# Sliding-window attention and gated MLP on one core: f32 scores without a q/k split, separate rooms, and a new instruction order

## Chip, cores and metric

One core of a Trainium2 chip. The metric is the device time of one execution in microseconds. The kernel before was timed in 3 runs: 453.04 us median, 451.68 to 454.27.

## What is computed

Attention over 4 batches, 8 heads, 768 positions and 64 columns per head. Each query sees the first 4 positions (the sink) and a window of 128. Then an MLP whose gate mixes positions. Cut from the reference:

```python
# attention, q, k, v: (4, 8, 768, 64)
scores = scale * np.matmul(q, k.transpose(0, 1, 3, 2))
keep = is_sink | in_window            # k < 4, or 0 <= q - k < 128
a = softmax(where(keep, scores, -1e9))
x = matmul(a, v)                      # -> (4, 768, 512)
# MLP
h = np.maximum(x @ w_in, 0.0)         # 512 -> 1024
u, v = h[..., :512], h[..., 512:]
v_n = (v - mu) / np.sqrt(var + 1e-06)
v_s = np.einsum('ts,bsd->btd', w_spatial, v_n) + b_spatial[None, :, None]
out = (u * v_s) @ w_out
```

All inputs are f32, w_in and w_out arrive as 64-bit floats and are decoded on the chip.

## The kernel before

**Precision.** Most products keep f32 precision by splitting each operand into a high and a low part: a cast gives the high part (`high`, L567 and L569), a subtraction the low part (`low` L583, `low_scaled` L590). `three` (L601) then multiplies high by high, high by low and low by high. This serves `ps_v` and `ps_u` (x times the two halves of w_in), `ps_s` (w_spatial times the normalised v, `vn`), `ps_o` (gate times w_out) and `av` (weights times values, L926 to L928). The scores (`sc`) of batches 1 to 3 are split in the same way (L856: three products from `qp` and `kring`). Those of batch 0 are multiplied as whole f32 from the loaded q and k (L850), which the simple switch `whole(b)` with `WHOLE = 1` decides.

**Tiling.** A batch has 6 tiles of 128 queries, and each tile has two halves of 4 heads. I number the 48 halves of the program from 0: half n is batch n // 12, tile (n % 12) // 2. For each half: the scores of 4 heads go to 4 PSUM banks (`sc` has exactly 4), VectorE adds the mask and takes the row's minimum (L861), ScalarE exponentiates (L866, 4 instructions per half), the weights are cast and split into `p` (ScalarE for the high part, VectorE or GpSimd for the low), two transposes on SP's DMA queue give `pT`, TensorE multiplies by the values, VectorE divides (L934 to L936), and x is split and transposed. Then come `ps_v` with relu (L969), statistics, normalisation and split on all four engines, and `ps_u` with relu (L1017). When all six tiles of a batch have their `vn`, the twelve pieces `ps_s` of a batch can run, each followed by the gate (L1038), the product with u (L1042) and the split of g; two `ps_o` per 256 columns end it.

**Rooms.** The block `wsp` (7 x 768 f32 per partition) holds w_spatial. Before w_spatial is loaded, the first part of it holds the raw v of batch 0 (`load_v`, L427) and the rest the k of batch 0 (`k_whole`). So the loads of w_spatial (L697) wait until batch 0 has used both (keys `v0room` and `k0room`).

**Order.** Every step is a piece given to `Plan.add` with a rank (its place in the program, from the table `WHEN`), the engines that may do it (`ENGINES`), a cost, and what it reads and writes. `Plan.order` sorts by rank, takes dependencies from that sorted list, and sends each piece to an engine. The engines then execute their lists strictly in that order. SP issues all loads, transposes and stores in one such list.

```python
plan.add(r, "PE", 0.19 + n / 2 * (1.0 if whole(b) else 0.35), product, ...)   # L869: scores
high(r, "q high", 512, lambda: (qp()[:, 0], raw()[:, 0]), ...)                # L815
low(r, "q low", 512, lambda: (qp()[:, 1], raw()[:, 0], qp()[:, 0]), ...)
plan.add(max(r0 + gap * c - 1, free_at), "SP", 0.37, f, [],                   # load of w_spatial
         [("wspraw", c), ("k0room", 0)] + [("v0room", t) for t in range(NT)], ...)
```

Of the kernel before, what the change touches and what calls it, by code (L numbers as in the profile page):

```python
# [6 lines left out]
F32 = mybir.dt.float32  # L7
F32R = mybir.dt.float32r
# [36 lines left out]
def f64_to_f32(nc, raw, w, tmp, top=None):  # L45


# [171 lines left out]
def scale_from_high_word(nc, pool, top, name):  # L219
# [23 lines left out]

ENGINES = {
# [34 lines left out]
class Plan:  # L279

# [8 lines left out]
    def add(self, rank, engines, time, f, reads=(), writes=(), dma=None, shared=False):  # L289

        self.pieces.append((rank, len(self.pieces), engines, time, f, tuple(reads), tuple(writes), dma, shared))

    def order(self):
        ps = sorted(self.pieces, key=lambda x: x[:2])
        n = len(ps)
        before, seen, users, takes = [set() for _ in ps], {}, {}, {}
        for i, (_, _, _, _, _, reads, writes, _, _) in enumerate(ps):
            for key, wr in [(k, False) for k in reads] + [(k, True) for k in writes]:
                base, part = key[:2], key[2:]
                if not wr and base not in seen and base[0] != "k0room":  # L300
# [33 lines left out]
        def room(i):  # L334

            t, new = 0.0, {}
            for key in ps[i][5] + ps[i][6]:
# [7 lines left out]
                j = new[ring] = new.get(ring, 0) + 1  # L345
                ends = sorted(until[b] if b else 0.0 for b in slots[ring] if b is None or not left[b])
# [821 lines left out]
```

## Time and profile before

| | |
|---|---|
| median of 3 runs | 453.04 us (451.68 to 454.27) |
| span of the profiled execution, first to last instruction | 451.5 us |
| TensorE busy | 401.8 us, 89% of the span |
| VectorE busy | 321.7 us, 71% |
| ScalarE busy | 296.4 us, 66% |
| GpSimd busy | 206.9 us, 46% |
| mean granted TensorE clock | 0.976 |

No time of the profiled execution other than its span was recorded; the span is 1.5 us below the median of the runs. The shares are means over a program whose first third and last two thirds behave differently, so they have to be read by stretches.

### The profile page before, as it was taken

The page shows a single profiled execution, that of the slowest core. Times are in us where ns is not written, and L with a number is a line of the kernel's source. Part 1 is how long each engine was busy: PE and PEld are TensorE (multiplying, and loading weights), DVE is VectorE, ACT ScalarE, POOL GpSimd, SP SyncE. Part 2 cuts the span into 40 slices and gives each one's busy share as a digit, 9 for nine tenths or more (in the row PEclk, how much of TensorE's full clock was granted, in tenths as well). Part 3 has the DMA queues.
Part 4 walks back from the last instruction along what each step waited for, and adds up shares of the span by engine and source line. Part 5 has one row for each costly group of instructions (what it writes and reads, how often), then busy time and mean ns, then how long its engine had stood idle before and what let it go on. Part 6 is the DMA issues. An engine that isn't in the chain of part 4 may idle for free.

```text
span 451.5 us, 10014 instructions
## 1 busy us (share of the span) xinstructions
PE 401.8 (89%) x3653; PEld 306.1 (68%) x3653; DVE 321.7 (71%) x953; ACT 296.4 (66%) x639; POOL 206.9 (46%) x275
## 2 busy tenths in 40 slices
PE   2364869986977999999999999999999999999995
PEld 1243537754564798787777877877788788778883
DVE  3999978889889898859789955687988453324220
ACT  4799768899899956749898565487876342331111
POOL 4446774477588595431356544232552242102220
PEclk9999979998888999999999999999999999999999
DMA  6998799899995537647987548547743444100102
GB/s 236 334 308 207 151 167 186 215 235 267 255 207 87 113 74 204 167 123 141 228 167 177 141 104 147 140 83 185 126 98 77 120 63 108 48 23 1 47 26 75
DMA packets 142393, 66.15 MB, mean 146 GB/s; under 512 B 124545, under 2 KB 128385, under 8 KB 142337
## 3 DMA queue, kind: packets, MB, share of 16 engines
q1 hardware_dynamic: 142192, 65.44, 62.7%
q8 instruction: 30, 0.49, 0.5%
q14 instruction: 27, 0.21, 0.2%
q10 hardware_dynamic: 144, 0.00, 0.0%
HBM read 28.72 MB, written 6.29 MB: 78 GB/s over the span
## 4 chain that ended last, share of the span: by engine, by line
PE 66%; DVE 12%; DMA 8%; ACT 6%; issue 3%; POOL 3%; SPq 2%; POOLq 0%; ACTq 0%; DVEq 0%
PE ps_s L601 21%; PE ps_o L601 14%; PE ps_v L601 10%; PE ps_u L601 9%; PE sc L856 5%; DVE pexp L861 3%; DMA xT<-x 2%; DMA wsp<-qk_t 2%; ACT pexp L866 2%; PE av L926 1%; DVE vring L590 1%; PE av L928 1%; PE av L927 1%; DVE win L590 1%; DMA dec<-w_in 1%
## 5 line engine op out<-in xcount | busy, mean ns | idle before, releaser
L601 PE MATMUL ps_s<-wsp,vn 128*128 128x256 f16 x864 | 100.2, 273 | 0.0
L601 PEld LDWEIGHTS <-vn 128*128 128x128 f16 x864 | 82.9, 98 | 13.8 <-issue 2.2
L866 ACT ACTIVATE pexp<-pexp,nm 128x260 f32<-128x260 f32 (+1 forms) x192 | 80.7, 483 | 11.1 <-DVE nm L861 10.7
L601 PE MATMUL ps_v<-win,xT 128*128 128x512 f16 x288 | 70.9, 399 | 4.6 <-DMA xT<-x 3.7
L601 PE MATMUL ps_u<-xT,win 128*128 128x256 f16 x576 | 70.8, 276 | 4.0 <-ACT vr L969 4.0
L601 PE MATMUL ps_o<-wout,g 128*128 128x512 f32 x288 | 73.0, 402 | 0.0
L601 PEld LDWEIGHTS <-win 128*128 128x128 f16 x576 | 55.1, 99 | 15.2 <-issue 6.7
L583 POOL TENSOR_TENSOR g<-g,g 128x256 fp32r<-128x256 f32 x48 | 39.0, 813 | 48.3 <-ACT g L567 47.1
L601 PEld LDWEIGHTS ps_o<-wout,g 128*128 128x128 f32 x288 | 52.3, 188 | 11.8 <-POOL g L583 0.3
L583 POOL TENSOR_TENSOR x<-x,x 128x256 f16<-128x256 f32 x48 | 38.6, 804 | 39.7 <-ACT x L567 39.0
L601 PEld LDWEIGHTS <-xT 128*128 128x128 f16 x288 | 27.7, 102 | 38.2 <-issue 7.4
L567 ACT CAST p<-pexp 128x1024 f16<-128x1024 f32 (+1 forms) x80 | 52.5, 669 | 0.3
L1038 DVE SCALAR_TENSOR_TENSOR g<-ps_s,isc,b_bc 128x256 f32<-128x256 f32 x48 | 23.1, 481 | 37.4 <-PE ps_s L601 37.2
L583 POOL TENSOR_TENSOR p<-pexp,p 128x16 f16<-128x16 f32 (+2 forms) x38 | 38.2, 1011 | 24.1 <-ACT p L567 20.7
L583 DVE TENSOR_TENSOR p<-pexp,p 128x1024 f16<-128x1024 f32 (+2 forms) x42 | 44.7, 1072 | 5.7 <-ACT p L567 5.7
L850 PE MATMUL sc<-wsp,qkraw 64*128 64x260 f32 (+1 forms) x96 | 23.0, 538 | 26.9 <-DMA wsp<-qk_t 9.9
L856 PE MATMUL sc<-kring,qp 64*128 64x260 f32 (+1 forms) x432 | 39.5, 307 | 3.7 <-DVE nm L861 3.7
L928 PE MATMUL av<-vring,pT 128*128 128x65 f16 x352 | 38.9, 198 | 2.8 <-DMA pT<-p 2.8
L927 PE MATMUL av<-vring,pT 128*128 128x65 f16 x352 | 39.0, 197 | 2.3 <-DVE vring L590 2.3
L856 PEld LDWEIGHTS sc<-kring,qp 64*128 64x128 f32 x432 | 30.9, 192 | 12.7 <-DVE nm L861 5.8
L1064 ACT COPY ob<-ps_o 128x512 f32<-128x512 f32 x24 | 14.0, 585 | 38.6 <-PE ps_o L601 38.6
L926 PE MATMUL av<-vring,pT 128*128 128x65 f16 x352 | 39.4, 198 | 0.0
(123 smaller groups left out, 707.2 us busy)
## 6 DMA issues: line engine op xcount, KB each, us to landing
qkraw<-qk_t SPq DMA_DIRECT2D x18, 512.0 KB, 4.1
out<-ob SPq DMA_DIRECT2D x24, 256.0 KB, 2.3
vraw<-v_s SPq DMA_DIRECT2D x18, 256.0 KB, 4.5
dec<-w_in SPq DMA_DIRECT2D x8, 512.0 KB, 6.7
wsp<-w_sp_t SPq DMA_DIRECT2D x6, 384.0 KB, 5.0
dec<-w_out SPq DMA_DIRECT2D x4, 512.0 KB, 4.8
wsp<-qk_t SPq DMA_DIRECT2D x6, 256.0 KB, 6.9
qkraw<-qk_t SPq DMA_DIRECT2D x6, 256.0 KB, 4.3
```

What stands on the lines that cost most here:

```text
L567: nc.scalar.copy(o, x)
L583: eng[e].tensor_tensor(out=o, in0=x, in1=hi, op=ALU.subtract)
L601: nc.tensor.matmul(o, a, m, start=(i == 0), stop=(i == n - 1))
L850: nc.tensor.matmul(o, tl("qkraw", (b, t))[rows, 0, hp, :], keys(k_whole, rows), start=True, stop=True)
L856: nc.tensor.matmul(o, qp[rows, qi, hp, :], keys(kring[:, ki], rows), start=(m == 0), stop=(m == 2))
L861: nc.vector.tensor_tensor_reduce(out=po, in0=o, in1=mask, scale=-0.125, scalar=3.0e38, op0=ALU.add, op1=ALU.min, accum_out=nm()[:, h2 + q: ...
L866: nc.scalar.activation(po, po, AF.Exp, bias=nm()[:, h2 + q:h2 + q + 1], scale=-1.0)
L926: nc.tensor.matmul(o[:, h], ph, vh, start=(t < 2 and j == 0), stop=False)
L927: nc.tensor.matmul(o[:, h], ph, vl, start=False, stop=False)
L928: nc.tensor.matmul(o[:, h], pl, vh, start=False, stop=(j == nb - 1 and (t < 2 or h == HH - 1)))
L1038: nc.vector.scalar_tensor_tensor(out=g(), in0=tl("ps_s", i)[:, :TC], scalar=vals["s", "sp"][1], in1=b_bc[:, t0:t0 + TC], op0=ALU.mult, op1 ...
L1064: plan.add(r + WHEN["o copy"], "a", 0.5, lambda e: nc.scalar.copy(tl("ob", i), tl("ps_o", i)), [("ps_o", i)], [("ob", i)])
```

## The change

Six things change.

1. `WHOLE`, `whole(b)`, the ring `qp` and the pieces "q high", "q low", "k high", "k low" go. All batches multiply whole f32 q and k (L803): 4 matmuls per half in place of 12. k is loaded straight into `kring` beside the two sink columns, in rows of 128 f32; q has a ring of 4.
2. `wsp` holds nothing but w_spatial, and the raw v of batch 0 is loaded like that of the other batches, tile by tile into the ring `vraw`. The keys `v0room` and `k0room` go, and with them the wait of the loads of w_spatial.
3. `Plan` takes dependencies from the order in which the pieces are listed; the rank only sets which goes first.
4. Most casts and low parts may now be done by more engines ("ad", "dp", "adp"), and the costs of the planner change.
5. The clamp of w_out goes from GpSimd to VectorE.
6. `WHEN` is a new table of numbers, with two values for each kind of piece (batch 0 and the others).

```diff
 ENGINES = {
-    "w_in high": "ap", "w_sp high": "ap", "v high": "a", "q high": "a", "k high": "a", "p high": "a",
...
+    "w_in high": "adp", "w_sp high": "adp", "v high": "ad", "p high": "ad", "sink high": "a", "x high": "adp",
...
-    "load": 5.69, "qk": 4.2, "k": 0.07, "score": 3.76, "pair": 0.43, "mask": 0.15, "exp": 0.99, "split": 1.0,
...
+    "qk load": (-1.47, 16.37), "k sink": (12.37, 77.34), "k copy": (-2.4, -12.82), "score": (-41.06, -9.59),
...
-WHOLE = 1
...
-        for i, (_, _, _, _, _, reads, writes, _, _) in enumerate(ps):
+        for _, k, _, _, _, reads, writes, _, _ in self.pieces:
+            i = place[k]
...
-    st.wsp = pool.tile([P, (NT + 1) * S], F32, name="wsp")
...
-    st.raw_v = [st.wsp[:, 512 * t:512 * t + 512] for t in range(NT)]
...
+        rooms = const.tile([P, NT + 1, S], F32, name="wsp")
...
-        kring = const.tile([P, 2, 4, HP, SEG], F32R, name="kring")
...
+        kring = const.tile([P, 4, HP, SEG], F32, name="kring")
...
-                    eng[e].tensor_scalar(w(), w(), EXP_LOW, EXP_HIGH, op0=ALU.max, op1=ALU.min)
+                    nc.vector.tensor_scalar(w(), w(), EXP_LOW, EXP_HIGH, op0=ALU.max, op1=ALU.min)
...
-                plan.add(max(r0 + gap * c - 1, free_at), "SP", 0.37, f, [],
-                         [("wspraw", c), ("k0room", 0)] + [("v0room", t) for t in range(NT)], dma=384 / 330.0)
...
+                plan.add("w_sp load", gap * c, 0, "SP", 0.37, f, [], [("wspraw", c)], dma=384 / 330.0)
...
-                    qp = tl("qp", (b, t))
-                    for m, (qi, ki) in enumerate(((0, 0), (0, 1), (1, 0))):
-                        for o, rows in zip(os, both):
-                            nc.tensor.matmul(o, qp[rows, qi, hp, :], keys(kring[:, ki], rows), start=(m == 0), stop=(m == 2))
...
+                        nc.tensor.matmul(view(h + q)[0], tl("q", (b, t))[rows, hp, :], keys, start=True, stop=True)
...
```

What each engine has to do between the exponentials of half 9 and those of half 20 (TensorE: from the scores of half 10 to those ahead of half 21), counted in the order of instructions of each kernel:

| engine | pieces | before | after |
|---|---|---|---|
| TensorE | scores of 4 heads | 9 split, 2 whole | 11 whole |
| | `ps_v`, `ps_u`, `ps_s`, `ps_o` | 6, 15, 0, 0 | 6, 16, 8, 1 |
| | matmuls of `av` | 222 | 247 |
| ScalarE | high parts of q and k | 13 | 0 |
| | sums of w_spatial (`junk<-wsp`), of v (`junk<-vraw`) | 6, 4 | 0, 9 |
| | high parts of p (1024), vn, g | 9, 6, 0 | 7, 3, 5 |
| | relu of v | 6 | 8 |
| VectorE | low parts of q and k | 6 | 0 |
| | gates, products with u, low parts of g | 0, 0, 0 | 8, 7, 5 |
| | low parts of x, w_out, vn | 0, 0, 4 | 4, 4, 1 |
| | casts of p, vn, w_out | 0 | 8 |
| | clamps and masks of decoded weights | 3 | 8 |

In the whole program GpSimd does 5 low parts of g in place of 48, 25 of x in place of 48, none of k in place of 13, and 14 of vn in place of 4.

First place: ScalarE, around the exponentials of half 16 (batch 1, tile 2). `junk` rows are the sums of w_spatial, `qp` and `kring` the high parts of q and k. Before:

```order
L700 ACTIVATE junk,mxs<-wsp 128x768
L567 CAST qp<-qkraw 128x512
L567 CAST kring<-qkraw 128x4x128
L866 ACTIVATE pexp<-pexp,nm 128x260 x4
L567 CAST x_1544<-x 128x256
L567 CAST p_1_135<-pexp 128x1024
L656 ACTIVATE w_1632<-dec 128x512
L658 ACTIVATE wtmp<-dec 128x512
L569 ACTIVATE vring<-vraw,v_scale 128x8x64
L700 ACTIVATE junk,mxs<-wsp 128x768
L969 ACTIVATE vr<-ps_v,icv_703 128x512
```

And now:

```order
L559 ACTIVATE vring<-vraw,v_scale 128x8x64 x2
L557 CAST x_1581<-x 128x256 x2
L813 ACTIVATE pexp<-pexp,nm 128x260
L916 ACTIVATE vr<-ps_v,icv_946 128x512
L813 ACTIVATE pexp<-pexp,nm 128x260
L557 CAST p_1_134<-pexp 128x1024
L956 ACTIVATE u<-ps_u,icu_605 128x256
L813 ACTIVATE pexp<-pexp,nm 128x260
L956 ACTIVATE u<-ps_u,icu_605 128x256
L813 ACTIVATE pexp<-pexp,nm 128x260
```

The sums of w_spatial and the casts of q and k are gone from here (the sums stand ahead of half 10 now), and the exponentials of one half are no longer issued in one go.

Second place: VectorE, behind the masks of half 18 (`ISA pexp` rows, not shown). Before, small sums and a division stand there:

```order
L625 TENSOR_REDUCE allmax_1866<-ps_row 1x1
L934 TENSOR_SCALAR den<-av 128x4
L935 RECIPROCAL den<-den 128x4
L936 TENSOR_TENSOR x<-av,den 128x256
L975 BN_STATS st<-vr 128x6
L977 BN_AGGR mv<-st 128x2
L979 TENSOR_SCALAR rs<-mv 128x1
L632 COPY allmax_r<-ps_col 128x1
```

And now:

```order
L639 TENSOR_SCALAR w_1796<-w_1796 128x512
L977 SCALAR_TENSOR_TENSOR g<-ps_s,isc,b_bc 128x256
L562 CAST wout<-w_1743 128x512
L981 TENSOR_TENSOR g<-g,u 128x256
L562 CAST p_1_134<-pexp 128x1024
L977 SCALAR_TENSOR_TENSOR g<-ps_s,isc,b_bc 128x256
L573 TENSOR_TENSOR wout<-w_1743,wout 128x512
L981 TENSOR_TENSOR g<-g,u 128x256
L881 TENSOR_SCALAR den<-av 128x4
```

Gates of batch 0 (`g<-ps_s`) stand ahead of the masks of half 19, with the decoding of w_out and a cast of p between them; in the kernel before, the first gate comes behind the masks of half 20.

Third place: SP's queue near the start, ahead of the first transposes of 8 blocks. Before, only loads of q, k and v stand there:

```order
L805 DMA wsp<-qk_t 128x4x128
L595 DMA vraw<-v_s 128x512 x4
L595 DMA vsraw<-v_sink 96x260
L712 DMA b_bc<-b_sp 128x768
L890 DMA_TRANSPOSE pT<-p_0_134 128x8x128 x2
```

And now:

```order
L774 DMA kring<-qk_t 128x4x128
L585 DMA q<-qk_t 128x512
L697 DMA b_bc<-b_sp 128x768
L585 DMA q<-qk_t 128x512
L683 DMA wsp<-w_sp_t 128x768 x3
L835 DMA_TRANSPOSE pT<-p_0_133 128x8x128 x2
```

Three of the six loads of w_spatial now come ahead of those transposes, where six loads of v of batch 1 stood.

## Rows read from the trace of the kernel before

**Rows 1.** The page: busy time of the engines, and two of the lines that cut the span into 40 slices of 11.3 us (busy tenths of TensorE, granted TensorE clock).

```profile
PE 401.8 (89%) x3653; PEld 306.1 (68%) x3653; DVE 321.7 (71%) x953; ACT 296.4 (66%) x639; POOL 206.9 (46%) x275
...
PE   2364869986977999999999999999999999999995
...
PEclk9999979998888999999999999999999999999999
```

**Rows 2.** Busy time by stretch (stretch, its length, then busy us and instructions of PE, PEld, DVE, ACT, POOL, the granted clock, the DMA share and GB/s).

```profile
10.00:62.00 52.00, 29.15 (x207) 19.54 (x206) 49.93 (x158) 45.56 (x100) 31.35 (x29) 0.99 0.98 245
62.00:71.50 9.50, 9.31 (x76) 5.16 (x77) 5.62 (x22) 4.10 (x10) 4.40 (x5) 0.69 0.64 134
71.50:151.30 79.80, 66.86 (x636) 46.74 (x633) 69.59 (x195) 73.71 (x161) 54.20 (x54) 0.91 0.97 206
151.30:332.00 180.70, 180.54 (x1803) 141.91 (x1802) 145.68 (x442) 130.87 (x288) 82.28 (x111) 1.00 0.65 146
332.00:451.50 119.50, 114.33 (x935) 91.44 (x932) 48.53 (x123) 38.68 (x83) 29.81 (x44) 0.99 0.24 60
```

**Rows 3.** The chain of waits that ended last, in order of time (start us, us, what): some of its TensorE pieces.

```profile
62.19 5.32 PE ps_v L601 x12
...
152.68 9.83 PE ps_s L601 x90
...
249.40 0.93 PE sc L856 x12
...
256.53 1.97 PE ps_s L601 x18
258.50 2.80 PE ps_o L601 x12
262.15 2.59 PE ps_v L601 x12
...
269.89 1.31 PE ps_u L601 x12
...
440.61 5.73 PE ps_o L601 x24
```

**Rows 4.** ScalarE's instructions in order of time (start us, duration us, line, what, count, and in brackets the idle time before and what ended it). The exponentials of half 9 are those at 69.79, the ones of half 20 those at 149.59.

```profile
67.53 0.69 ACT L969 ACTIVATE vr<-ps_v,icv 128x512 f32<-128x512 f32 x1 [3.80 <-PE ps_v L601]
69.79 1.72 ACT L866 ACTIVATE pexp<-pexp,nm 128x260 f32<-128x260 f32 x4 [1.57 <-DVE nm L861]
...
72.06 0.62 ACT L567 CAST vn<-vr 128x512 f16<-128x512 f32 x1
72.58 1.04 ACT L567 CAST p<-pexp 128x1024 f16<-128x1024 f32 x1
73.53 0.40 ACT L567 CAST x<-x 128x256 f16<-128x256 f32 x1
...
149.59 1.71 ACT L866 ACTIVATE pexp<-pexp,nm 128x260 f32<-128x260 f32 x4
```

**Rows 5.** TensorE in order of time: two groups of whole f32 scores of batch 0 with what follows them (each f32 matmul leaves two records), and two neighbouring matmuls of `av`.

```profile
53.15 1.15 PE L850 MATMUL sc<-wsp,qkraw 64*128 64x260 f32 x8
54.23 0.28 PE L920 MATMUL av<-vsink,pT 96*128 96x260 f16 x1
...
54.87 0.19 PE L928 MATMUL av<-vring,pT 128*128 128x65 f16 x1
54.90 0.19 PE L926 MATMUL av<-vring,pT 128*128 128x65 f16 x1
...
71.80 1.15 PE L850 MATMUL sc<-wsp,qkraw 64*128 64x260 f32 x8
72.88 2.76 PE L601 MATMUL ps_v<-win,xT 128*128 128x512 f16 x12
```

**Rows 6.** VectorE's instructions in order of time.

```profile
92.28 0.68 DVE L583 TENSOR_TENSOR qp<-qkraw,qp 128x512 fp32r<-128x512 f32 x1
92.88 0.42 DVE L861 CUSTOM_DVE_ANT_0 pexp<-sc,m_second 128x260 f32<-128x260 f32 x1
...
93.22 0.43 DVE L861 CUSTOM_DVE_ANT_0 pexp<-sc,m_second 128x260 f32<-128x260 f32 x1
...
98.19 1.84 DVE L590 SCALAR_TENSOR_TENSOR vring<-vraw,v_scale,vring 128x512 f16<-128x512 f32 x1
```

**Rows 7.** GpSimd's instruction at the moment of the last of these rows.

```profile
98.22 1.26 POOL L667 TENSOR_TENSOR w<-w,wtmp 128x512 int32<-128x512 int32 x1 [1.12 <-DVE w L664]
```

**Rows 8.** Groups of instructions by line and form (count, then busy us in all, mean ns of one, idle us before them and what ended it).

```profile
L567 ACT CAST qp<-qkraw 128x512 fp32r<-128x512 f32 x18 | 11.1, 614 | 3.3 <-PE sc L856 3.3
L700 ACT ACTIVATE junk<-wsp 128x768 bf16<-128x768 f32 x6 | 5.0, 841 | 1.1 <-DMA wsp<-w_sp_t 1.0
L583 DVE TENSOR_TENSOR p<-pexp,p 128x1024 f16<-128x1024 f32 x28 | 36.7, 1312 | 3.6 <-ACT p L567 3.6
L1042 DVE TENSOR_TENSOR g<-g,u 128x256 f32<-128x256 f32 x48 | 25.1, 523 | 0.8
L662 DVE TENSOR_SCALAR w<-w 128x512 int32<-128x512 int32 x12 | 7.4, 622 | 1.5 <-POOL w L652 1.4
L1038 DVE SCALAR_TENSOR_TENSOR g<-ps_s,isc,b_bc 128x256 f32<-128x256 f32 x48 | 23.1, 481 | 37.4 <-PE ps_s L601 37.2
```

**Rows 9.** DMA issues (count, KB each, median us from issue to landing).

```profile
qkraw<-qk_t SPq DMA_DIRECT2D x18, 512.0 KB, 4.1
...
wsp<-w_sp_t SPq DMA_DIRECT2D x6, 384.0 KB, 5.0
wsp<-qk_t SPq DMA_DIRECT2D x6, 256.0 KB, 6.9
```

More of the change, by code (lines that the diff above doesn't have):

```diff
@@ L260 @@
-    "w_in 1 gap": 0.0, "w_in 0 gap": 0.28, "w_sp gap": 0.39, "w_out gap": 2.14,
+    "qk load": (-1.47, 16.37), "k sink": (12.37, 77.34), "k copy": (-2.4, -12.82), "score": (-41.06, -9.59),
+    "mask": (-3.75, -4.01), "exp": (-17.07, 31.97), "p high": (-2.13, 3.59), "turn high": (36.35, -26.36),
+    "sink high": (50.94, 37.26), "sink low": (-1.35, 30.72), "p low": (-0.16, 61.38), "turn low": (-43.61, -0.01),
[3 rows of a table added]
+    "ps_v": (-104.28, -63.22), "v relu": (3.25, -23.63), "icv": (50.22, 52.95), "icu": (-43.54, -1.4),
@@ new lines @@
+    "v stats": (3.01, 113.55), "v root": (-26.61, -33.27), "v norm": (-79.73, 111.22), "vn high": (-0.22, 48.2),
+    "vn low": (66.38, 55.49), "ps_u": (46.35, 7.74), "u relu": (-2.57, 18.51), "ps_s": (16.63, 16.3),
+    "gate": (-39.62, -18.46), "times": (-11.47, -13.48), "g high": (-2.12, -47.94), "g low": (-44.68, 30.91),
+    "ps_o": (21.78, 21.75), "o copy": (-16.27, -41.2), "o store": (52.66, 71.31), "w_in 1 load": (-24.98, -63.54),
+    "w_in 1": (-1.93, -2.41), "w_in 1 split": (-4.16, -14.81), "w_in 0 load": (5.05, 12.41), "w_in 0": (-0.87, 31.77),
@@ L576, in f, with low @@
                     nc.gpsimd.tensor_scalar(o, x, 1.0 if sc is None else sc, 1.0, op0=ALU.mult, op1=ALU.mult)
-            plan.add(rank, ENGINES[kind], costs(kind, n, pointer=scale is not None), f, reads, writes, shared=True)
-        def low(rank, kind, n, views, reads, writes):
+            plan.add(name, step, b, ENGINES[kind], costs(kind, n, pointer=scale is not None), f, reads, writes, shared=True)
+        def low(name, step, b, kind, n, views, reads, writes):
             def f(e):
@@ L583, in f, with low_scaled @@
                 eng[e].tensor_tensor(out=o, in0=x, in1=hi, op=ALU.subtract)
[L584 to L586 removed]
+            plan.add(name, step, b, ENGINES[kind], costs(kind, n, two=True), f, reads, writes, shared=True)
+        def low_scaled(name, step, b, n, views, scale, reads, writes):
             def f(e):
@@ L828, in scores @@
-        def scores(i, b, t, hf, h2, r, n):
-            outs = lambda q: tl("sc", (i, h2 + q))[:, :2 * SEG].rearrange("p (a c) -> p a c", a=2)
+            room, ks = kring[:, kslot(b, t)], f"kslot{kslot(b, t)}"
+            rl = early(f"q {t}", "qk load", r, b)
+            plan.add(*rl, b, "SP", 0.37, lambda e: nc.sync.dma_start(room[:, :, 2:], qk[b, t, 1]),
+                     [], [(ks, i, 0)], dma=256 / 330.0)
+            load(*rl, b, "q", i, lambda: qk[b, t, 0], 256)
+            if t == 0:
+                plan.add("k sink", r, b, "p", 0.2, lambda e: nc.gpsimd.tensor_copy(ksink, room[:, :, 2:2 + NS]),
+                         [(ks, i, 0)], [("ksink", b)])
```

511 lines of the change are left out of this document (224 added, 287 removed), and 6 rows, old and new, of tables (ENGINES, WHEN).

## The prediction

> **What bounds the kernel now.** I first read the slices of the page [rows 1]: TensorE is full from the fourteenth slice (153 us) to the end and has holes before it. So the program is two programs, and I split it by stretches [rows 2].
>
> How much work is in it? Hot pieces of TensorE follow one another at 1.97 us for `ps_s` (18 matmuls), 2.80 for `ps_o`, 2.59 for `ps_v`, 1.31 for `ps_u`, 0.93 for the split scores of 4 heads [rows 3], 1.08 for whole f32 scores (start to start) and 0.03 for a matmul of `av` [rows 5]. By the counts in the code: 48 x 1.97 + 24 x 2.80 + 24 x 2.59 + 48 x 1.31 + 1088 x 0.03 + 3 (sink matmuls) + 30 x 0.93 + 10 x 1.08 + 12 halves of first tiles at about 0.55 (half the columns, an estimate from these rows) = 366 us. The profiled span is 451.5, so 86 us hold no TensorE work at its hot pace.
>
> Where? By the exponentials of half 20, which end at 151.3 [rows 4], the order has put 75 us of TensorE work ahead. So 76 of the 86 us are lost by then. The remaining 290 us of pieces take 300.2 us, a factor of 1.035 with the end included (the last matmuls stop at 446.3 [rows 3]). Behind 151 us TensorE is the bound. Only the time before can be won.
>
> What sets it there? From 10 to 62 us VectorE works 49.9 of 52 us. From 62 to 71.5 both VectorE and ScalarE stand still much of the time: ScalarE waits 3.80 us for a `ps_v` [rows 4] that runs at the 1.2 GHz level, 5.32 us [rows 3], where the granted clock is 0.69 [rows 2]. From 71.5 to 151.3 (exponentials of half 9 to those of half 20) ScalarE works 73.7 of 79.8 us, VectorE 69.6, and TensorE's pieces in it are worth only 52.5 us hot. ScalarE is the bound there, VectorE the next.
>
> **The cost of each part.** I use *own times*: the time from an instruction's start to the next one's start when nothing holds it. On ScalarE that is the shown duration less 0.1 (the cast of vn is 0.62, the next starts 0.52 later [rows 4]), on VectorE less 0.08 (0.68 and 0.60 for the low part of q, 0.42 and 0.35 for a mask [rows 6]).
>
> *Scores on TensorE.* 30 groups of 1.08 in place of 0.93 [rows 3, 5], plus 6 first tiles at about 0.07 more: +5 us, nearly all in the part where TensorE is the bound. What the rows show is a group of 260 columns that costs 16% more. The Trainium skill, page "FP8 and Floating Point Precision", section "TensorE Precision Notes", counts 4 passes for a true f32 product; against 3 split products that would be 4/3 of 0.93, 1.24 a group, and +10 us. The trace has the group itself, and I take its 1.08.
>
> *First stretch, to half 9.* By the order, ScalarE has 51.0 us of own time ahead (52.3 before), VectorE 48.8 (48.9): the sums of w_spatial come in, the relus of two `ps_v` go behind half 10. So the hole from 62 to 71.5 loses its cause; I take 3.5 us off (the wait of 3.80) and let half 9 end at 68. Bounds: 66 to 71.5. TensorE has 20.7 us ahead instead of 22.8.
>
> *Second stretch, half 9 to half 20.* ScalarE: 13 high parts of q and k (0.52 each, from 0.614 [rows 8]) -6.8, six sums of w_spatial with their read-out -5.6 [rows 8], two high parts of p -1.9, three of vn -1.6; five more sums of v +3.6, five high parts of g +1.5, two relus +1.2, small ones -0.9: 73.1 becomes 62.6. VectorE: low parts of q and k -3.7, of vn -1.8; 8 gates (0.40) +3.2, 7 products with u (0.35 undisturbed, 0.523 on average) +2.4, 9 low parts of g and x +3.1, 4 of w_out +2.5, 5 clamps and masks (0.39) +1.9, the 8 casts +3.9, and 3.8 for two more tiles' statistics, splits of v and w_spatial and the rest: 55.0 becomes 70.3. A cast of p on VectorE has no row: 512 elements with one source take 0.46 undisturbed, 1024 with two sources 1.31 on average [rows 8]; I take 0.65 between them, nearer to the one-source row, and the three cast 1.2 to 3.4 us in all. TensorE: 74.3 us instead of 52.5, since eight `ps_s` are ready (the loads of w_spatial stand ahead of half 4 and no longer behind batch 0).
>
> So VectorE takes ScalarE's place. Its own time stretches when GpSimd works beside it: a split of v that took 1.84 us ran beside GpSimd's 1.26 [rows 6, 7]. Busy time over own time was 49.9/42.5 = 1.17 from 10 to 62 us with GpSimd busy 60% of it, 69.6/55.0 = 1.27 from 71.5 with 68%, and 145.7/127.8 = 1.14 from 151.3 to 332 with 46% [rows 2]. GpSimd's own work over these tiles falls by a quarter (40.7 to 31.0 us by the order: no low part of k, no clamp of w_out, fewer of x), to about half of the stretch. I take 1.15, which gives 81 us, and 2 us of waits: the stretch takes 83 us and ends at 151, as before, but with 95 us of TensorE work done instead of 75. Bounds: 77 (TensorE's 74.3 x 1.035) and 89 (factor 1.27).
>
> *The rest.* TensorE has 370.5 - 95.0 = 275.5 us left, x 1.035 = 285. VectorE's own time from half 20 to half 44 is 109.0 us, x 1.15 = 125, while TensorE's pieces there need 123.2 x 1.035 = 127.5: level, where VectorE had room before. For two engines this close I add 3.5 us of waits (bounds 0 and 5). The casts that ScalarE gives up and the low parts that GpSimd gives up are covered as long as VectorE keeps up; if it doesn't, they cost what VectorE is late.
>
> *Sum:* 68 + 83 + 285 + 3.5 = 439.5 against the span of 451.5. The median of the runs is 1.5 us above the span, so **441 us**, 2.7% less. By 151 us TensorE has done 20 us more than before; 5 of these pay for the f32 scores and 3.5 for the waits.
>
> **Rivals.**
>
> *VectorE becomes the bound to the end: slower.* For it: it gets 15 us more in the second stretch, and its 1.27 there is a measured factor. With 1.27 from half 9 to half 44: 71.5 + 89 + 138 + 157.6 (TensorE's last 152.3 us) = 456, a median of 457.5. It decides from a factor of 1.24 over both stretches. Against it: GpSimd's work shrinks, and 1.14 held over 181 us at 46%. The Trainium skill, "GPSIMD Engine Reference", section "Specifications", says that GpSimd shares its SBUF interfaces with VectorE instructions that have two SBUF inputs or run in a two-port mode. By that rule the added low parts, products and casts are the kind that collide; rows 6 and 7 agree.
>
> *VectorE does not bind: faster still.* If collisions fall with GpSimd's work to 1.06, the second stretch is TensorE's 77 us and no waits follow: 68 + 77 + 285 = 430, a median of 431.5.
>
> *The transfers take the gain: no change.* The DMA engines are 97 to 98% busy to 151 us [rows 2]. Three loads of w_spatial, 5.0 us each, come ahead of the transposes of halves 2 and 3, and k in rows of 512 B lands after 6.9 us for 256 KB where q and k together, 512 KB, took 4.1 [rows 9]. One load's wait at the start and one of 4 us in the second stretch: 441 + 9 = 450. Against it: the bytes ahead of the first 8-block transposes are the same within 0.1 MB, as six loads of v move behind. It covers also a change that does nothing it says; the order shows the splits gone and the loads ahead, so that alone is not likely.
>
> **How the numbers follow.** The forecast 0.57, the faster rival 0.17, the transfers 0.13, the slower rival 0.13. Anything within 0.5% (450.8 to 455.3) cannot be told from no change here. The forecast and the faster rival lie below it, and 0.05 of the transfers: 0.79 faster. 0.07 of the transfers and 0.02 of the slower rival are the same: 0.09. The rest, 0.12, is slower. The range: the low end is the faster rival, 431. The high end takes the bounds 71.5 + 89 + 285 + 4.5 = 450 of span, 451 of median. Outside stay the slower rival and a little on each side.
>
> **What would show it.** Right: the group of whole f32 scores at about 1.08 us; the exponentials of half 20 near 151 us with the first `ps_s` at about 115 to 125 us instead of 152.7; ScalarE under 85% busy and VectorE over 90% from half 9 to half 20; TensorE's slices full from the eleventh or twelfth on; VectorE's busy time around 340 us in all and GpSimd's under 160. Wrong: exponentials of half 20 after 160 us, or TensorE waiting for VectorE's masks or gates by more than 10 us behind half 20 (the slower rival), or waits for `pT`, `xT` or `kring` of more than 10 us in the first 150 us (the transfers), or a score group above 1.2 us.

## The result, and the profile after

The changed kernel takes **440.38 us** (median of 4 runs, 439.9 to 440.74), the kernel before beside it 453.43 (451.68 to 454.27). The ratio is 0.9736, with a 95% interval of 0.9698 to 0.9773: 2.6% less time. The forecast was 441, with a range of 431 to 451. The profiled span is 438.5 us, where 439.5 was forecast and the kernel before has 451.5.

The page of the changed kernel, the same lines as [rows 1] (busy time, TensorE's slices of 11 us, the granted clock):

```profile
PE 400.7 (91%) x3509; PEld 301.9 (69%) x3509; DVE 330.2 (75%) x1048; ACT 252.8 (58%) x561; POOL 129.7 (30%) x192
...
PE   1537897899899999999999999999999999999995
...
PEclk9999988999999999999999999999999999999998
```

TensorE is full from the twelfth slice on, where it was from the fourteenth. ScalarE gave up 44 us, GpSimd 77, VectorE took 8.5 more.

By stretch, cut where the exponentials of half 9, half 20 and half 44 end (columns as in [rows 2]):

```profile
10.00:62.00 52.00, 34.88 (x217) 22.05 (x215) 48.51 (x163) 45.79 (x105) 26.35 (x25) 0.97 1.08 277
62.00:66.40 4.40, 4.40 (x43) 2.45 (x43) 4.33 (x16) 2.93 (x8) 0.00 (x0) 1.00 1.12 234
66.40:150.80 84.40, 78.20 (x733) 57.52 (x732) 78.23 (x234) 64.82 (x146) 37.02 (x47) 0.98 0.83 181
150.80:279.20 128.40, 128.40 (x1330) 94.75 (x1329) 118.65 (x416) 99.83 (x229) 52.16 (x73) 1.00 0.94 190
279.20:438.50 159.30, 153.81 (x1187) 124.12 (x1185) 78.19 (x210) 36.69 (x72) 9.24 (x13) 0.99 0.23 57
```

The third row is the stretch that the forecast turned on, half 9 to half 20. It ends about where it ended before (150.8 us, 151.3 before), but TensorE was busy 78.2 us in it, at a clock of 0.98. Before, it was busy 66.9 us at 0.91 in 79.8 us [rows 2].

ScalarE in order of time, as [rows 4]; the last exponentials of half 9 and those of half 20:

```profile
64.72 1.72 ACT L813 ACTIVATE pexp<-pexp,nm 128x260 f32<-128x260 f32 x4 [1.41 <-DVE nm L808]
...
149.05 1.73 ACT L813 ACTIVATE pexp<-pexp,nm 128x260 f32<-128x260 f32 x4 [0.84 <-DVE nm L808]
```

VectorE's last low part of vn of batch 0, and TensorE around the first `ps_s`, which answers to 152.68 in [rows 3]; the two rows of TensorE also give a group of whole f32 scores hot, from 119.59 to 120.67, as in [rows 5]:

```profile
118.68 0.68 DVE L573 TENSOR_TENSOR vn<-vr,vn 128x512 f16<-128x512 f32 x1
```

```profile
119.59 1.15 PE L803 MATMUL sc<-kring,q 64*128 64x260 f32 x8
120.67 2.58 PE L591 MATMUL ps_s<-wsp,vn 128*128 128x256 f16 x22
```

Groups that answer to [rows 8] (count, busy us, mean ns, idle before), the cast of p on VectorE among them, which had no row before:

```profile
L573 DVE TENSOR_TENSOR p<-pexp,p 128x1024 f16<-128x1024 f32 x26 | 31.7, 1220 | 0.0
...
L977 DVE SCALAR_TENSOR_TENSOR g<-ps_s,isc,b_bc 128x256 f32<-128x256 f32 x48 | 23.2, 483 | 41.2 <-PE ps_s L591 40.9
...
L981 DVE TENSOR_TENSOR g<-g,u 128x256 f32<-128x256 f32 x45 | 20.1, 447 | 0.9
...
L562 DVE CAST p<-pexp 128x1024 f16<-128x1024 f32 x12 | 8.3, 688 | 0.7 <-ACT pexp L813 0.7
```

**Where the time came from.** I add up the matmuls that had started by a time at the hot costs of the forecast, and call the rest of that time lost to TensorE. For the groups of first tiles I take what the traces show, 0.65 us whole and 0.82 split, where the forecast had estimated 0.55. Before, 54.6 us were lost by 100 us, 74.2 by 150 and 84.2 in all. After, 54.7 were lost by 100, 57.8 by 150 and 67.7 in all. So 16.5 us less are lost, all of them between 100 and 150 us. 3.5 us of added f32 work go against that, which leaves the 13.0 us of the spans. The two windows from 100 to 150 us show it, before and after:

```profile
100.00:150.00 50.00, 39.26 (x353) 27.91 (x353) 43.40 (x113) 46.49 (x98) 36.33 (x32) 0.86 0.93 204
```

```profile
100.00:150.00 50.00, 48.19 (x434) 36.48 (x434) 46.25 (x132) 36.79 (x82) 22.97 (x26) 1.00 0.76 164
```

Before, TensorE waited and ran at a granted clock of 0.86. After, it hardly waits and stays at 2.4 GHz.

### The profile page after: what moved, and what is told of

It is laid out like the page before. It is cut to its first block, busy times and chain, and to the rows that moved or that the text cites. A ratio compares the mean times of both kernels' runs of the same rounds, so it can differ in the third digit from the quotient of the medians.

```text
span 438.5 us, 9688 instructions
## 1 busy us (share of the span) xinstructions
PE 400.7 (91%) x3509; PEld 301.9 (69%) x3509; DVE 330.2 (75%) x1048; ACT 252.8 (58%) x561; POOL 129.7 (30%) x192
## 4 chain that ended last, share of the span: by engine, by line
PE 75%; DVE 13%; DMA 5%; ACT 2%; issue 2%; SPq 1%; ACTq 0%; DVEq 0%
PE ps_s L591 22%; PE ps_o L591 16%; PE ps_u L591 12%; PE ps_v L591 11%; PE sc L803 8%; DVE pexp L808 3%; PE av L873 2%; PE av L874 2%; PE av L875 2%; DMA q<-qk_t 1%; DMA dec<-w_in 1%; DMA vraw<-v_s 1%; DMA dec<-w_out 1%; DVE p L573 1%; DVE vring L580 1%
## 5 line engine op out<-in xcount | busy, mean ns | idle before, releaser
L813 ACT ACTIVATE pexp<-pexp,nm 128x260 f32<-128x260 f32 (+1 forms) x192 | 82.7, 484 | 11.1 <-DVE nm L808 10.5
L803 PE MATMUL sc<-kring,q 64*128 64x260 f32 (+1 forms) x384 | 65.6, 427 | 13.8 <-DMA q<-qk_t 9.2
L591 PE MATMUL ps_o<-wout,g 128*128 128x512 f32 x288 | 71.0, 400 | 0.0
L591 PE MATMUL ps_v<-win,xT 128*128 128x512 f16 x288 | 68.4, 391 | 0.8 <-DVE allmax_r L619 0.5
L803 PEld LDWEIGHTS sc<-kring,q 64*128 64x128 f32 x384 | 39.8, 204 | 28.5 <-DVE nm L808 9.2
L573 POOL TENSOR_TENSOR p<-pexp,p 128x16 f16<-128x16 f32 (+2 forms) x43 | 41.9, 981 | 43.7 <-ACT p L557 36.4
L1004 ACT COPY ob<-ps_o 128x512 f32<-128x512 f32 x24 | 14.0, 585 | 66.9 <-PE ps_o L591 66.0
L591 PEld LDWEIGHTS <-xT 128*128 128x128 f16 x288 | 28.2, 100 | 34.2 <-issue 6.3
L956 ACT ACTIVATE u<-ps_u,icu 128x256 f32<-128x256 f32 x48 | 22.7, 472 | 40.4 <-PE ps_u L591 39.8
L557 ACT CAST p<-pexp 128x32 f16<-128x32 f32 (+2 forms) x65 | 37.6, 599 | 0.8 <-DMA pT<-p 0.5
L573 DVE TENSOR_TENSOR p<-pexp,p 128x1024 f16<-128x1024 f32 (+2 forms) x37 | 36.3, 989 | 0.3 <-ACT p L557 0.3
L873 PEld LDWEIGHTS <-pT 128*128 128x128 f16 x352 | 33.4, 100 | 3.2 <-issue 2.4
L874 PEld LDWEIGHTS <-pT 128*128 128x128 f16 x352 | 33.3, 100 | 1.8 <-issue 0.8
```

Of the source, the lines that this page charges most:

```text
L557: nc.scalar.copy(o, x)
L573: eng[e].tensor_tensor(out=o, in0=x, in1=hi, op=ALU.subtract)
L591: nc.tensor.matmul(o, a, m, start=(i == 0), stop=(i == n - 1))
L803: nc.tensor.matmul(view(h + q)[0], tl("q", (b, t))[rows, hp, :], keys, start=True, stop=True)
L813: nc.scalar.activation(po, po, AF.Exp, bias=nm()[:, q:q + 1], scale=-1.0)
L873: nc.tensor.matmul(o[:, h], ph, vh, start=(t < 2 and j == 0), stop=False)
```

## The experiments

Theory at the start: TensorE's loss ends because several parts together let it have more work before 150 us, in a stretch where ScalarE was the bound and VectorE now is. Rivals: one part alone pays (f32 scores, separate rooms, lists, order), or some other engine binds. All runs in one table. The ratio is to the kernel before, timed beside each; "lost" is TensorE's lost time as above (left out where the scores are bf16).

| kernel | us | ratio (95%) | first `ps_s` | half 20 ends | lost by 100, by 150 | span |
|---|---|---|---|---|---|---|
| before | 453.4 | 1 | 152.5 | 151.3 | 54.6, 74.2 | 451.5 |
| changed | 440.4 | 0.974 (0.970 to 0.977) | 120.7 | 150.8 | 54.7, 57.8 | 438.5 |
| before_f32 | 455.4 | 1.007 (1.004 to 1.010) | 155.2 | 140.1 | 55.5, 72.9 | 454.2 |
| old_order | 461.3 | 1.022 (1.015 to 1.029) | 134.4 | 154.0 | 60.3, 72.4 | 456.9 |
| old_order2 | 461.6 | 1.025 (1.021 to 1.028) | 132.5 | 148.3 | 59.9, 72.6 | 458.8 |
| late_wsp | 449.0 | 0.994 (0.991 to 0.998) | 125.8 | 160.4 | 54.7, 65.3 | 447.2 |
| old_lists | 448.5 | 0.994 (0.991 to 0.998) | 128.0 | 159.2 | 58.4, 65.8 | 447.1 |
| casts_to_act | 448.1 | 0.993 (0.990 to 0.995) | 127.7 | 157.8 | 58.5, 64.7 | 446.5 |
| lows_to_pool | 443.1 | 0.983 (0.980 to 0.986) | 120.6 | 150.7 | 53.0, 57.8 | 438.6 |
| act_casts | 439.6 | 0.975 (0.967 to 0.983) | 120.3 | 150.5 | 52.5, 57.4 | 438.3 |
| dve_lows | 458.4 | 1.015 (1.010 to 1.020) | 123.9 | 155.0 | 54.8, 60.9 | 455.0 |
| short_lows | 440.6 | 0.974 (0.968 to 0.980) | 121.5 | 151.6 | 55.2, 58.8 | 439.9 |
| one_product | 429.2 | 0.951 (0.946 to 0.957) | 119.4 | 148.8 | | 426.4 |
| both_less | 431.9 | 0.955 (0.950 to 0.961) | 121.4 | 150.8 | | 431.4 |

### One part alone: f32 scores in the kernel before

```diff
-WHOLE = 1
+WHOLE = 4
-        kring = const.tile([P, 2, 4, HP, SEG], F32R, name="kring")
+        kring = const.tile([P, 4, HP, SEG], F32, name="kring")
...
-                room = k_whole[:, kslot(b, t)]
+                room = (kring if b else k_whole)[:, kslot(b, t)]
```

> The kernel before with whole f32 scores in all four batches and nothing else of the change: its own table of ranks, engine lists and shared room of w_spatial stay; the q ring has 4 places of half the size, the split pieces go. Theory (the gain comes from several parts that only together let TensorE start its ps_s pieces early): the 13 casts of q and k leave ScalarE between half 9 and half 20 (6.8 us), half 20 comes some 5 us earlier, the f32 groups take 4 to 5 us back behind it, and w_spatial is still split at about 145 us, so that no ps_s runs before that: 447 to 453 us, a few us below the kernel before at most. Rival (freeing ScalarE of the casts is the gain): 443 us or less.

Measured: 455.4 us, 0.7% slower, 2 us beyond the theory's range and far from the rival. Half 20 came 11 us earlier (140.1), so dropping the split does speed up the halves. But nothing was ready for TensorE to fill the time with: w_spatial is still split at the end of the stretch, and `ps_s` follows it. VectorE's last split of w_spatial and TensorE's first `ps_s` in this kernel:

```profile
153.13 1.02 DVE L590 SCALAR_TENSOR_TENSOR wsp<-wsp,wsp_scale 128x768 f16<-128x768 f32 x1 [0.17 <-ACT wsp L569]
```

```profile
155.24 0.93 PE L601 MATMUL ps_s<-wsp,vn 128*128 128x256 f16 x7
```

ScalarE did not become free either: with the casts gone, it was still busy 45.2 of the 50 us from 100 on (46.5 before), as other work moved up. The f32 scores alone buy 0.8 us of lost time (84.2 to 83.4) and cost 3.5 us of work.

### All but the order: the ranks of the kernel before

```diff
-    "qk load": (-1.47, 16.37), "k sink": (12.37, 77.34), "k copy": (-2.4, -12.82), "score": (-41.06, -9.59),
...
-    "w_in 0 split": (0.57, -27.68), "w_sp load": (36.8, 29.12), "w_sp sum": (50.05, -61.75),
...
-GAP = {"o": 0.201, "s": 0.751, "u": 1.654, "v sum": 1.920, "w_in 0": 0.416, "w_in 1": 0.266, "w_out": 1.377, "w_sp": 0.683}
+WHEN = {"qk load": [-5.69], "k sink": [-4.2], "k copy": [-4.2], "score": [-3.76], ...
... "w_sp load": [2.5], "w_sp sum": [3.5], "w_sp split": [5.84], ...
+GAP = {"o": 0.24, "s": 0.67, "u": 0.67, "v sum": 0.1, "w_in 0": 0.28, "w_in 1": 0.0, "w_out": 2.14, "w_sp": 0.39}
```

> The changed kernel with the ranks of the kernel before, carried over to the new table piece by piece: f32 scores, own rooms, the wider engine lists and dependencies from the listing stay. The order puts 83 us of TensorE work ahead of the exponentials of half 20 (6 ps_s) where the changed kernel has 95 (8 ps_s) and the kernel before 75 (none). Theory: the time follows the work that TensorE has ahead of half 20, so between the two, 445 to 452 us. Rival 1 (the new table of ranks is worth nothing): 440 to 443. Rival 2 (the new table is the whole gain): 453 or more.

Measured: 461.3 us, rival 2 and beyond: 2.2% slower than the kernel before. With f32 scores, rooms and lists all there, the old ranks give about the loss of the kernel before (86.1 us in all, 84.2 there) and add the 3.5 us of f32 work. One doubt remained: the old ranks put w_spatial earlier than the kernel before could load it, and batch 0 suffered (half 9 ended at 77.9 instead of 66.4). So I gave w_spatial later ranks, and left the rest of the old ones. Cut out of the new table, where the run above had 2.5, 3.5 and 5.84:

```diff
... "w_sp load": [8.74], "w_sp sum": [8.74], "w_sp split": [11.08], ...
```

> As the run with the ranks of the kernel before, but with those of w_spatial as late as the kernel before really had them (behind batch 0's use of the room, its loads at rank 8.74 instead of 2.5), so that they don't push batch 0 back. Ahead of half 21 stand 4 ps_s and 77 us of TensorE work. Theory (the order as a whole decides how much TensorE has to do before 150 us): 452 to 460 us, so the old order loses the gain wherever w_spatial stands. Rival (only the too early w_spatial made the old ranks slow): 440 to 447 us.

Measured: 461.6 us, as the theory had it, 1.6 above its range. But w_spatial did not come as late as in the kernel before. The loads and low parts of w_spatial in this kernel (count, shortest, median and longest ns, first and last start in us):

```profile
L666 SPq DMA_DIRECT2D wsp<-w_sp_t x6: 327/328/430, 29.2 to 45.0; - x6
L563 DVE SCALAR_TENSOR_TENSOR wsp<-wsp,wsp_scale x6: 1001/1010/2257, 100.9 to 123.2; 128x768 f16<-128x768 f32 x6
```

The loads came from 28.2 to 35.4 us in old_order and from 80.9 to 118.1 in the kernel before, the low parts from 80.8 to 95.8 and from 134.2 to 149.7. So the splits moved by some 20 us, the loads hardly, and half 9 still ended at 76.8. In the changed kernel the loads are as early (28.0 to 51.5) and half 9 ends at 66.4, so early loads alone don't hold batch 0 back. Without the new order the other parts gain nothing with w_spatial's splits at either place; loads as late as in the kernel before were not run. The old ranks belong to other parts, so this is no price of the order by itself: the runs show that it is needed, not that it would do alone.

### The new order with one part taken away

```diff
-                plan.add("w_sp load", gap * c, 0, "SP", 0.37, f, [], [("wspraw", c)], dma=384 / 330.0)
+                plan.add("w_sp load", gap * c, 0, "SP", 0.37, f, [("used", 0)], [("wspraw", c)], dma=384 / 330.0)
...
-            plan.add("score", i, b, "PE", 1.0 if t else 0.54, product, [("q", (b, t))] + keys, banks)
+            plan.add("score", i, b, "PE", 1.0 if t else 0.54, product, [("q", (b, t))] + keys, banks + ([("used", 0, i)] if b == 0 else []))
...
+            if b == 1:
+                w_spatial()
+                gates(0)
...
```

> The changed kernel with the loads of w_spatial held back, in the list that orders the pieces, until the scores of batch 0 are done, as in the kernel before; everything else of the change stays, the order is planned anew. In the changed kernel w_spatial is split by 107 us and the first ps_s starts at 120.7, right behind the last vn of batch 0 (119.4); in the kernel before the last vn came at about 139 and the split at 151. Theory: with the rest of the change w_spatial has 13 us to spare, and loads behind batch 0's scores use up about that: first ps_s at 121 to 130 us, 440 to 446 us in all. Rival (the separate rooms are what lets ps_s start early): first ps_s behind 140 us and 450 us or more.

Measured: the mechanism as the theory had it (first `ps_s` at 125.8), the time not: 449.0, 3 us above its range. w_spatial now comes in beside batch 1, and half 20 ends 10 us later. The loss by 100 us is that of the changed kernel (54.7); 7.5 us more are lost by 150. The order was planned anew, so not all of this need be w_spatial's: half 9 ends at 72.2, where the changed kernel has 66.4. So the separate rooms don't decide when `ps_s` can start. They let w_spatial's 6 sums and 12 splits be done where other work leaves room.

```diff
+                if kind in ("p high", "vn high", "v high", "w_out high"):
+                    e = "a"
+                elif kind in ("x high", "g high", "w_in high", "w_sp high") and e == "d":
+                    e = "a"
...
+                if kind in ("g low", "x low", "w_out low"):
+                    e = "p"
...
-                eng[e].tensor_tensor(out=g(), in0=g(), in1=tl("u", (b, c0))[:, d, :], op=ALU.mult)
+                nc.vector.tensor_tensor(out=g(), in0=g(), in1=tl("u", (b, c0))[:, d, :], op=ALU.mult)
```

> The changed kernel in its own order, but each cast and low part on the one engine that the lists of the kernel before allow: high parts on ScalarE wherever VectorE had them, low parts of x, g and w_out all on GpSimd, products with u all on VectorE. Theory: lists alone are a small part, since between half 9 and half 20 ScalarE would get about 5 us more (67.6 of 84 us) and VectorE 7 us less: 442 to 448 us. Rival (shifting work to VectorE is the gain): 451 us or more. A second rival, that VectorE is the bound so hard that giving it less helps: below 438.

Measured: 448.5 us, just above the theory (442 to 448), so the lists are worth 8 us. Which half of them? First the high parts alone (in `high`), then the low parts alone (in `low`).

```diff
+                if e == "d":
+                    e = "a"
```

> The changed kernel in its own order, with every high part that VectorE makes (12 casts of p of 0.69 us, 28 of g, those of vn, v, x and the weights) made by ScalarE instead, which had room for 36 extra casts at no cost; the low parts stay where they are. Theory (TensorE is the bound from about 80 us on, VectorE only keeps up with it): no gain, 438 to 442 us. Rival 1 (VectorE binds between half 9 and half 20): 437 us or less. Rival 2 (the wider lists for the high parts are what lost 8 us when all lists were narrowed): 446 us or more.

```diff
+                if kind in ("g low", "x low", "w_out low"):
+                    e = "p"
```

> The other half of the narrowed lists: the changed kernel in its own order, with the low parts of x, g and w_out that VectorE makes (23, 43 and 4) all on GpSimd, the high parts where the change has them. Theory (GpSimd's low part of x takes 0.79 us where VectorE's takes 0.42, and it lies on the way from x to ps_v and vn): nearly all of the 8 us of the narrowed lists, 445 to 450 us. Rival (it was the high parts): 439 to 442 us.

Measured: 448.1 and 443.1 us, the reverse of what I expected: it was the high parts. The low parts on GpSimd leave the profiled span at 438.6, but that run is the fastest of the four (the others have spans of 440.7 to 441.9). Their median is 0.9% above the changed kernel's own ratio, so 3 to 4 us there stay open. The chain of waits of casts_to_act shows how a cast on ScalarE costs (start us, us, what):

```profile
72.19 1.31 ACT pexp L815 x3
73.50 0.93 ACT p L559
74.44 0.41 ACT pexp L815
...
74.96 0.59 ACT vr L918
...
75.59 4.78 PE ps_v L593 x12
```

In the changed kernel the cast of that half runs on VectorE from 70.76, for 0.60 us on the chain. Here it stands ahead of an exponential and of the relu that frees the PSUM bank of `ps_v`. TensorE has waited by then, and the `ps_v` of 2.59 us hot takes 4.78, at the 1.2 GHz level. The windows 60 to 75 and 75 to 81 us of this kernel, with granted clocks of 0.73 and 0.61:

```profile
60.00:75.00 15.00, 12.54 (x108) 8.05 (x106) 11.36 (x42) 12.30 (x31) 0.22 (x1) 0.73 1.03 205
75.00:81.00 6.00, 5.41 (x34) 2.39 (x34) 4.58 (x14) 2.06 (x4) 2.81 (x5) 0.61 0.77 176
```

In the changed kernel the clocks there are 0.89 and 1.00, and the same `ps_v` takes 3.75 us. From 60 to 80 us casts_to_act loses 9.4 us (45.2 to 54.6), the changed kernel 6.5.

### What binds the changed kernel

Four kernels keep its order and change what one engine has to do, and a fifth changes two. First two extra casts per tile of batches 1 to 3 on ScalarE, then two extra subtractions per tile on VectorE, on constants, ahead of the tile's masks and exponentials:

```diff
...
+                if b and not hf:
+                    for _ in range(2):
+                        nc.scalar.copy(extra_out, extra[:, 0])
```

> The same on ScalarE: two extra casts of 128x512 (0.52 us each) ahead of the exponentials of each tile of batches 1 to 3, on constants, for the time that the high parts of q and k took. Between half 9 and half 20 that is 10 of them, 5.2 us on an engine that is busy 64.7 of 84.3 us. Theory (ScalarE is no longer what binds, VectorE is): 440 to 442.5 us. Rival (the unloaded ScalarE by itself is what pays): 445 us or more.

```diff
...
+                if b and not hf:
+                    for _ in range(2):
+                        nc.vector.tensor_tensor(out=extra_out, in0=extra[:, 0], in1=extra[:, 1], op=ALU.subtract)
```

> The changed kernel in its own order, with two extra subtractions of 128x512 on VectorE ahead of the masks of each tile of batches 1 to 3, on constants and into a tile that nobody reads: the time that the low parts of q and k took, 36 of about 0.6 us, without their dependencies. Theory (VectorE is the bound between half 9 and half 20 and level with TensorE behind it): 10 of them, 6 to 7 us, lie ahead of half 20, which moves from 150.8 to 154 to 158 us; behind it VectorE has 9.7 us of 128 to spare up to half 44 for another 14 to 16 us: 446 to 453 us. Rival (VectorE has room for them): 443 us or less.

Measured: 439.6 us, so 36 casts on ScalarE cost nothing that stands clear of the interval (0.967 to 0.983), as the theory had it. And 458.4 us, 5 above the theory's range: 21.6 us of work on VectorE (36 of 0.60 us) cost 16.5 us of span, 18 of the medians. dve_lows by stretch, half 9 to half 20 and on to half 44:

```profile
66.60:155.00 88.40, 79.33 (x755) 58.75 (x753) 83.06 (x243) 64.78 (x146) 35.54 (x47) 0.98 0.80 172
155.00:296.50 141.50, 134.36 (x1325) 98.82 (x1321) 137.99 (x440) 98.09 (x229) 57.46 (x73) 1.00 0.85 174
```

In the second row stand 24 of the subtractions, 14.4 us by own time, and the stretch grew by 13.1 us, not by the 5 or 6 that would be left if VectorE's 9.7 us without work could be filled. VectorE's busy time grew by 19.3 us (118.65 to 137.99), more than the work put in, and its time without work only fell to 3.5. So what looked like room was not there for other work; I read it as collisions and waits.

Now less work. TensorE reads q and k as bf16, or VectorE's low parts of p are cut short (the rest of the tile is cleared once at the start), or both:

```diff
+        def halves(x):
+            return x.bitcast(BF16)
...
-                        nc.tensor.matmul(view(h + q)[0], tl("q", (b, t))[rows, hp, :], keys, start=True, stop=True)
...
+                        nc.tensor.matmul(view(h + q)[0], halves(tl("q", (b, t)))[rows, hp, 1::2],
+                                         keys[..., 1::2], start=True, stop=True)
```

> The changed kernel in its own order, with each score matmul reading q and k as bf16 (the upper halves of the f32 words, in strides of 2), which makes the scores coarse: it stands for less TensorE work. If a group takes 0.45 us instead of 1.08, some 28 us of TensorE work go, 15 of them between half 20 and half 44 and 2 behind. Theory (VectorE and TensorE are level there, VectorE 118.7 us busy of 128.4): the stretch from half 20 to half 44 shrinks by 5 to 9 us, the one before by at most 2: 428 to 434 us. Rival (TensorE alone is the bound behind half 20, VectorE has room): 416 to 425 us.

```diff
-            nc.gpsimd.memset(t[:, 4 * HH], 0.0)
+            nc.vector.memset(t, 0.0)
...
+                if kind == "p low" and e == "d":
+                    o, x, hi = o[..., :16], x[..., :16], hi[..., :16]
```

> The changed kernel in its own order, with the low parts of p that VectorE makes cut to an eighth of their elements (the rest of the tile is cleared once at the start): 26 subtractions of 1.22 us become about 0.2, eight of them between half 9 and half 20. It stands for a VectorE with 8 us less to do in that stretch. Theory (VectorE binds there): half 20 moves from 150.8 to 143 to 148 us, and TensorE, full behind it, gives that on: 432 to 436 us. Rival (something else binds, such as the chain of waits through ScalarE and the transposes): 439 to 441 us.

> The short low parts of p on VectorE and the bf16 scores on TensorE together, in the changed kernel's own order: each engine alone had some 8 us less to do between half 9 and half 20, and alone neither moved half 20 by more than 2 us (84.4 us for that stretch in the changed kernel, 83.8 with the short low parts, 82.0 with the bf16 scores, whose group takes 0.34 us). Theory (the two engines are level, so that only relief of both shows): 76 to 79 us for the stretch, 113 to 118 us from half 20 to half 44 (128.4 in the changed kernel, 120.3 with bf16 scores), 416 to 423 us in all. Rival (the stretch is set by a chain of waits through ScalarE, the transposes and GpSimd): 81 us or more for the stretch, and 425 us or more in all.

Measured: one_product 429.2 us, inside the theory's 428 to 434. A group takes 0.34 us, some 16 us of TensorE's work left the stretch from half 20 to half 44, and the stretch fell by 8.1 us (128.4 to 120.3), with VectorE busy 117.2 of it. From half 9 to half 20 it fell by only 2.4 us (84.4 to 82.0):

```profile
66.80:148.80 82.00, 73.47 (x710) 52.40 (x707) 77.84 (x234) 64.07 (x147) 37.52 (x47) 0.96 0.87 183
148.80:269.10 120.30, 114.84 (x1233) 81.82 (x1229) 117.21 (x416) 97.66 (x230) 54.79 (x73) 1.00 0.99 200
```

short_lows gave nothing: 440.6 us where the theory had 432 to 436, so here the rival holds. From half 9 to half 20 VectorE was busy only 72.3 us, TensorE still 78.3, and half 20 ended no sooner:

```profile
67.80:151.60 83.80, 78.28 (x761) 58.53 (x759) 72.29 (x235) 64.62 (x146) 34.32 (x47) 1.00 0.85 184
```

And both together gave no more than the one: 431.9 us, the rival again. From half 9 to half 20 it took 83.4 us, so relief of both engines does not shorten that stretch either. The same two stretches of both_less, and TensorE's longest waits in them (what waited, for what, us, times, longest):

```profile
67.40:150.80 83.40, 73.98 (x731) 53.19 (x729) 74.29 (x235) 64.51 (x147) 33.87 (x47) 0.96 0.83 183
150.80:273.80 123.00, 115.28 (x1230) 81.88 (x1228) 104.82 (x414) 97.89 (x229) 50.36 (x73) 0.99 1.01 196
```

```profile
PE ps_v L593 <- DMA xT<-x: 4.6, 4, 2.0
PE sc L808 <- DVE nm L814: 3.9, 2, 2.3
PE av L873 <- DMA pT<-p: 3.8, 3, 3.3
PE av L881 <- DMA pT<-p: 2.3, 1, 2.3
```

No engine is over 94% busy in either row. TensorE waits 10.7 us for transposed tiles there, where the changed kernel waits 2.3 in the same stretches, and the DMA engines are at 0.83 and 1.01 (0.83 and 0.94). So in this fixed order the next thing behind TensorE and VectorE is the way through the transposes. That reading rests on waits and shares. No kernel here changed the transposes alone.

## Why the prediction was right

**Size of the stretches: right.** First stretch 66.4 us (forecast 68). Second 84.4 us, ending at 150.8 (83, ending at 151). The rest 287.7 (285 and 3.5). First `ps_s` at 120.7 (115 to 125). ScalarE 77% busy from half 9 to half 20 (under 85), VectorE 93% (over 90). VectorE 330 us in all (340), GpSimd 130 (under 160). Two slips of the forecast moved none of this: its 366 us of work counts 12 halves of first tiles, but there are 8 (the sum is the one with 8), and the DMA engines were not 97 to 98% busy all the way to 151 us, since [rows 2] has 0.64 from 62 to 71.5.

**f32 scores: right for the full groups.** A group takes 1.08 us. A first tile's takes 0.65 where the split one took 0.82, so 0.17 less and not 0.07 more, and the added work is 3.5 us against 5. First the split one of the kernel before with what follows it, then the whole one of the changed kernel:

```profile
178.70 0.89 PE L856 MATMUL sc<-kring,qp 64*128 64x128 f32 x12
179.52 0.72 PE L601 MATMUL ps_s<-wsp,vn 128*128 128x256 f16 x5
```

```profile
80.61 0.71 PE L803 MATMUL sc<-kring,q 64*128 64x128 f32 x8
81.25 0.28 PE L867 MATMUL av<-vsink,pT 96*128 96x260 f16 x1
```

By the forecast's estimate, the Trainium skill's four passes ("FP8 and Floating Point Precision", "TensorE Precision Notes") would have made 1.24 for a full group; the measured group decides.

**VectorE in ScalarE's place: the term was mis-sized in two ways that cancel.** I took 70.3 us of own time, a factor of 1.15 and 2 us of waits. VectorE was busy 78.2 us, a factor of 1.11, and stood still for 6.2. Behind half 20 the factor was 1.09 (118.65 over 109.0). GpSimd was busy 44% and 41% of these stretches, so they continue the series that the forecast read before: 1.27 at 68%, 1.17 at 60%, 1.14 at 46%. In lows_to_pool 13 low parts leave VectorE in that stretch, 5.5 us by own time. VectorE is busy 78.45 us all the same, a factor of 1.21 with GpSimd at 56%.

```profile
65.30:150.70 85.40, 79.59 (x735) 58.35 (x736) 78.45 (x221) 64.87 (x146) 47.99 (x60) 0.98 0.78 178
```

**What binds that stretch: half right.** More work on VectorE makes the program longer (dve_lows), but less makes it no shorter (short_lows). So the step from VectorE's stretched own time to the length of the stretch does not hold by itself. TensorE, 78.2 of 84.4 us busy, which I had put at 77 as the lower end, is not what is left: with less on TensorE the stretch took 82.0 us (one_product), with less on both 83.4 (both_less). What else holds it there, a chain of waits by the theory's rival, stays open, and that 83 came out at 84.4 is in part luck. My rival of a VectorE that doesn't bind priced that at 431.5 us; with less on VectorE the time stayed at 440.6.

**Level behind half 20: right, and tighter than said; the sum has misses that cancel.** TensorE waits for nothing behind 150.8, so the 3.5 us of waits that I added did not come. In their place more work was left: by the costs above TensorE had done 92.9 us by half 20 and not 95, 15.8 more than the kernel before (77.1 by 151.3) and not 20. For the remaining 277.9 us (275.5 forecast) it took 287.7, the forecast's factor of 1.035. The f32 scores added 3.5 us and not 5. That the sum came within 1 us of the span is in part luck. As for level: 14.4 us more on VectorE cost 13.1.

**What the argument did not see: how much hangs on the order.** I counted the pieces as the new order has them and priced them. That gave the right sum, but the text reads as if unloading ScalarE were the source. The runs speak against that: ScalarE's casts can come back at no cost (act_casts), while the f32 scores alone cost time (before_f32), and all parts without the order end 21 us above the changed kernel (old_order). What the missing split saves in the new order is VectorE's time: 36 low parts there are 16.5 us of span. That is the most it can be, since in the kernel before VectorE made 23 of the 36 and GpSimd 13. No kernel here has the new order with the split scores, or the rooms or the lists alone in the kernel before, so what the order, the rooms and the lists are each worth by themselves is not shown.

**The transfers did not take the gain.** TensorE's waits for `pT` from 66 to 279 us are 2.3 us. With the first loads of q and k, for which it stands 9.0 us at the very start, waits for `pT` and `kring` come to 11.6 us by 150, over the 10 that I had set as a sign. But the kernel before also stands there for its first loads (7.4 and 6.8 us), and by 60 us both have lost the same, 44.7 us before and 45.1 after.

## What to carry to other kernels

Where an order is planned for an in-order machine, parts of a change are not worth what they are worth one by one: here f32 scores alone came out 0.7% slower than the kernel before, all without the lists or with late loads 0.6% faster, all without the order 2.2 to 2.5% slower, and all together 2.6% faster. Ask of each engine both questions, what more work costs and what less work gives; here they had different answers for VectorE, which stands nearly level with TensorE. A cast that is free on an engine with room is not free when it stands ahead of what TensorE waits for.

## What the runs showed of the chip

- VectorE's busy time over its own time (as the forecast counts it) follows GpSimd's share: 1.09 at 41%, 1.11 at 44%, 1.21 at 56%, beside the 1.14 to 1.27 of the kernel before. Moving 13 low parts to GpSimd from half 9 to half 20 gave VectorE nothing back (78.2 us busy and 78.45).
- Four score matmuls of 260 columns take 1.08 us in f32 and 0.34 us when they read every second bf16 of the same bytes.
- Short waits of TensorE are paid twice: from 100 to 150 us the granted clock was 0.86 before and 1.00 after, and a `ps_v` that takes 2.59 us at 2.4 GHz took 4.78 behind a wait.
